# Output weights folded by 32-column products, epsilon as a 29th column, whole-bank gate steps: a linear-attention and GEGLU block

## The chip, the cores and the metric

One NeuronCore of a Trainium2 chip runs the whole program in one launch. The metric is the device time of one execution in microseconds (us); the kernel before took 190.51 us as a median of three runs (190.48 to 190.52). The profile is of one execution and counts from the first to the last instruction, its span.

## What is computed

A pre-norm attention block with linear attention and a gated feed-forward block, each with a residual, over 2048 tokens of 448 features. All inputs are bf16.

```python
def _A_ref(x, wqkv, wo):                     # B, S, D = 1, 2048, 448
    H = 16; Dh = D // H                      # 16 heads of 28
    q, k, v = split(x @ wqkv)
    phi = lambda t: jnp.where(t > 0, t + 1, jnp.exp(t)) + 1e-6
    pq, pk = phi(q), phi(k)
    kv = jnp.einsum("bhsd,bhse->bhde", pk, v)
    z = jnp.einsum("bhsd->bhd", pk)
    num = jnp.einsum("bhqd,bhde->bhqe", pq, kv)
    den = jnp.einsum("bhqd,bhd->bhq", pq, z)[..., None] + 1e-6
    return merge_heads(num / den) @ wo

def _B_ref(x, w_gate, w_up, w_down):         # Df = 1792
    h = _gelu(x @ w_gate) * (x @ w_up)
    return h @ w_down

h = x + _A_ref(_layernorm(x), A_wqkv, A_wo)
h2 = h + _B_ref(_layernorm(h), B_w_gate, B_w_up, B_w_down)
```

## The kernel before

The tokens are 16 tiles of 128. The program has three stages, all under one hand-made order.

**First stage, keys and queries.** Each tile is normalised, transposed (by PE for four tiles, by DMA for twelve) and multiplied by the key or the query weights (`k_t` and `q_t`, L469, four matmuls of 448 columns). Keys become `pk` on ACT and DVE (L480 to L482). The products `pt_t` (L488) accumulate the transposed normalised tile times `pk` over all tokens in four PSUM banks; a column of ones in the tile gives the sums `z`. The q groups are not all needed early: PE fills waits with them.

**Middle.** The sums leave PSUM: `z` to ACT (L514) and a copy to the other half of the partitions (L515, DVE), the four parts of `pt` by DVE (L516, L521) and ACT (L519). `kv` (L527) multiplies them by the value weights, 16 small matmuls. DVE masks the result head by head (`kvm`, L531) into a sheet of zeros and copies 64 columns of it once more (`kvd`, L536). Seven products (L547) of 128 columns of that sheet with the output weights give the folded weights `w2`: four groups of 128 rows, evicted by ACT (L551) and DVE (L553). Two DMAs also store them with the halves of the partitions exchanged. From then on the attention of a tile is one matrix product.

**The denominators.** DVE finishes the queries (L564 and L565 for a tile, L582 and L583 for a pair). The queries times `z` go to the tile `t1` (L569 or L585, mostly on POOL), DVE sums 28 columns per head (L572 or L586), ACT adds epsilon (L574 or L588), DVE inverts (L575 or L589) and scales the queries (L576 or L590). The first pair of tiles is transposed by PE and evicted by ACT (L599, L602), the others by DMA. `out1` (L617) multiplies the first pair by `w2`; `outA` and `outB` (L627, L628) do it for the other pairs on two halves of the array's rows.

**Feed-forward.** DVE adds the residual (L633), the second layer norm follows (L413, L414; L645 or L662), PE (L654) or DMA transposes. In `gu` steps, L731 (gate, lower 64 rows of the array) and L733 (up, upper 64 rows) run as pairs over seven pieces of the contraction. A step fills one PSUM bank of 512 columns for each: for the chunks of two tiles it has two 128-wide pieces of the hidden width and 256 tokens, for the chunks of four tiles one piece and 512 tokens. Two banks for each alternate. ACT takes the gelu of the bank in two halves (L751), DVE multiplies by the up product in two halves (L753). `down` steps (L697, L678) multiply by the down weights; DVE adds the residual (L707, L682) and SP stores (L708, L683). The last tile is done in two column halves, each with its own add and store.

**What sets the order.** Every operation is recorded as a task with the tasks that it waits for. `ORDERS` lists, for each engine, the task numbers in the order in which they are issued; an engine issues in that order, and a waiting instruction holds those behind it. `HOLD` names, for a task that waits for several others, which of the waits comes first. Both are tables of numbers, and both were written anew for the change because fewer tasks exist.

The lines on which the change bears:

```python
BK_KV, BK_W2 = 4, (5, 6, 7, 4)
gs = (c, c + 1) if c < 3 else (3,)          # w2: one or two products per group of 128 rows
for hh_ in range(2):                        # the gate and the product, a half bank each
```

Of the kernel before, what the change touches and what calls it, by code (L numbers as in the profile page):

```python
# [6 lines left out]
F32 = mybir.dt.float32  # L7
# [41 lines left out]
)  # L49
HOLD = {  # L50
    66: (36,), 141: (140,), 165: (164,), 214: (213,), 216: (215,), 323: (302,), 326: (324,), 431: (340,), 704:
    (564,), 735: (734,), 781: (672,), 839: (836,), 849: (846,), 854: (852,), 866: (865,),
# [176 lines left out]
def bass_sequential_preLN__linear_attn_block__glu_gated_geglu__prompt_kernel(  # L229
# [17 lines left out]
    G = _Graph()  # L247
    es = ExitStack()
    with es:
# [573 lines left out]
```

## Time and profile before

| what | value |
|---|---|
| median of three runs | 190.51 us (190.48 to 190.52) |
| span of the profiled execution | 188.3 us |
| granted clock of PE | 1.000 throughout |
| ACT gates (L751), 112 of 256 columns | 36.6 us, 383 ns each |
| DVE products (L753), 112 of 256 columns | 42.1 us, 416 ns each |
| PE gate and up matmuls (L731, L733), 490 each | 88.6 and 88.8 us, side by side |

The three runs carry no span of their own; the profiled execution's time is its span, and 2.2 us of the runs' median lie outside it. Busy time of PE counts overlapping tails of matmuls, so starts are read rather than lengths. Matmuls on 64 rows of the array appear as pairs at the same time. The rest of the profile is shown where the prediction reads it.

### The profile page before, as it was taken

The page shows a single profiled execution, that of the slowest core. Times are in us where ns is not written, and L with a number is a line of the kernel's source. Part 1 is how long each engine was busy: PE and PEld are TensorE (multiplying, and loading weights), DVE is VectorE, ACT ScalarE, POOL GpSimd, SP SyncE. Part 2 cuts the span into 40 slices and gives each one's busy share as a digit, 9 for nine tenths or more (in the row PEclk, how much of TensorE's full clock was granted, in tenths as well). Part 3 has the DMA queues.
Part 4 walks back from the last instruction along what each step waited for, and adds up shares of the span by engine and source line. Part 5 has one row for each costly group of instructions (what it writes and reads, how often), then busy time and mean ns, then how long its engine had stood idle before and what let it go on. Part 6 is the DMA issues. An engine that isn't in the chain of part 4 may idle for free.

```text
span 188.3 us, 4459 instructions
## 1 busy us (share of the span) xinstructions
PE 184.3 (98%) x1813; PEld 109.2 (58%) x1813; DVE 129.3 (69%) x330; ACT 76.5 (41%) x220; POOL 50.0 (27%) x91
## 2 busy tenths in 40 slices
PE   7999999999999999999999999999999999999994
PEld 7545555555688788965554555555545545454554
DVE  4999959999899998786796762562645244335432
ACT  3878752799963231432234222321242222224100
POOL 6067910704505686033614000206100000000000
PEclk9999999999999999999999999999999999999999
DMA  5996458999393526820005720000096000002024
GB/s 169 387 231 88 96 104 194 218 222 174 65 320 64 95 52 116 84 52 0 0 3 98 144 54 0 0 3 2 3 135 111 3 0 24 3 0 98 3 79 140
DMA packets 35076, 17.11 MB, mean 91 GB/s; under 512 B 26864, under 2 KB 33648, under 8 KB 35056
## 3 DMA queue, kind: packets, MB, share of 16 engines
q1 hardware_dynamic: 34432, 16.32, 41.1%
q10 hardware_dynamic: 624, 0.52, 0.8%
q8 instruction: 14, 0.23, 0.5%
q14 instruction: 6, 0.05, 0.1%
HBM read 8.26 MB, written 1.84 MB: 54 GB/s over the span
## 4 chain that ended last, share of the span: by engine, by line
PE 94%; DVE 3%; DMA 1%; issue 0%
PE ps L733 38%; PE ps L697 19%; PE ps L469 12%; PE ps L731 9%; PE ps L488 6%; PE ps L627 3%; PE ps L678 3%; PE ps L628 2%; DMA x_sb<-in_A_x_dram 1%; DVE st L413 1%; PE ps L617 1%; PE ps L547 1%; PE ps L527 1%; PE ps L443 0%; PE ps L654 0%; DVE den L572 0%
## 5 line engine op out<-in xcount | busy, mean ns | idle before, releaser
L733 PE MATMUL ps<-hnT,wgu_sb 64*128 64x512 bf16 (+1 forms) x490 | 88.8, 333 | 0.0
L731 PE MATMUL ps<-hnT,wgu_sb 64*128 64x512 bf16 (+1 forms) x490 | 88.6, 333 | 0.0
L751 ACT ACTIVATE gl<-ps 128x256 bf16<-128x256 f32 x112 | 36.6, 383 | 85.3 <-PE ps L731 84.4
L753 DVE TENSOR_TENSOR hh<-ps,gl 128x256 bf16<-128x256 f32 x112 | 42.1, 416 | 41.4 <-ACT gl L751 41.3
L733 PEld LDWEIGHTS ps<-hnT,wgu_sb 64*128 64x128 bf16 x490 | 45.2, 94 | 32.9 <-DVE hh L753 3.4
L731 PEld LDWEIGHTS ps<-hnT,wgu_sb 64*128 64x128 bf16 x490 | 45.4, 94 | 2.5
L697 PE MATMUL ps<-wd_sb,hh 64*128 64x448 bf16 x392 | 41.5, 349 | 0.0
L697 PEld LDWEIGHTS ps<-wd_sb,hh 64*128 64x128 bf16 x392 | 23.2, 94 | 14.5
L469 PE MATMUL ps<-wqk_sb,xnT 128*128 128x448 bf16 x128 | 27.4, 353 | 0.0
L413 DVE BATCH_NORM_STATS2 st<-x_sb 128x6 f32<-128x448 bf16 x32 | 19.2, 612 | 1.8 <-DMA x_sb<-in_A_x_dram 1.7
L585 POOL TENSOR_TENSOR t<-pq,zbc 128x448 f32<-128x448 bf16 x12 | 12.3, 1042 | 23.7 <-DVE pq L583 22.0
L469 PEld LDWEIGHTS ps<-wqk_sb,xnT 128*128 128x128 bf16 x128 | 11.9, 98 | 11.4 <-DVE pk L482 0.8
L488 PE MATMUL ps<-pk,xnn 128*128 128x448 bf16 x64 | 13.9, 352 | 0.0
L627 PE MATMUL ps<-w,pqnT 64*128 64x448 bf16 x49 | 11.5, 349 | 0.1
L425 POOL TENSOR_SCALAR ln<-mv 128x2 f32<-128x2 f32 x7 | 2.0, 291 | 35.2 <-DVE mv L414 35.0
L480 ACT ACTIVATE e<-ps 128x448 bf16<-128x448 f32 x16 | 8.5, 539 | 5.6 <-PE ps L469 5.5
L628 PE MATMUL ps<-pt_sb,pqnT 64*128 64x448 bf16 x42 | 10.2, 350 | 0.0
L633 DVE TENSOR_TENSOR x_sb<-ps,x_sb 128x448 bf16<-128x448 f32 x16 | 9.6, 616 | 0.7 <-PE ps L628 0.6
L662 POOL TENSOR_SCALAR hn<-x_sb,nm,rs 128x448 bf16<-128x448 bf16 x14 | 9.9, 719 | 0.4
L482 DVE SCALAR_TENSOR_TENSOR pk<-ps,e 128x448 bf16<-128x448 f32 x16 | 9.8, 617 | 0.1
L488 PEld LDWEIGHTS ps<-pk,xnn 128*128 128x128 bf16 x64 | 6.3, 98 | 5.9 <-DVE pk L482 0.3
L453 POOL TENSOR_SCALAR xnn<-x_sb,nm,rs 128x448 bf16<-128x448 bf16 x12 | 8.9, 744 | 2.2 <-ACT rs L422 1.9
(85 smaller groups left out, 160.5 us busy)
## 6 DMA issues: line engine op xcount, KB each, us to landing
out_dram<-x_sb SPq DMA_DIRECT2D x15, 112.0 KB, 1.8
wd_sb<-in_B_w_down_dram SPq DMA_DIRECT2D x1, 1568.0 KB, 8.4
x_sb<-in_A_x_dram SPq DMA_DIRECT2D x3, 448.0 KB, 5.9
wgu_sb<-in_B_w_gate_dram SPq DMA_DIRECT2D x1, 896.0 KB, 12.1
wgu_sb<-in_B_w_up_dram SPq DMA_DIRECT2D x1, 896.0 KB, 16.5
wgu_sb<-in_B_w_gate_dram SPq DMA_DIRECT2D x1, 672.0 KB, 6.1
wgu_sb<-in_B_w_up_dram SPq DMA_DIRECT2D x1, 672.0 KB, 8.5
wo_sb<-in_A_wo_dram SPq DMA_DIRECT2D x1, 392.0 KB, 7.5
```

The source lines that it names most:

```text
L413: op("dve", lambda e: e.bn_stats(st[:, t, :], src_ap), [b_src], [b_st[t]], "bnst%s_%d" % (tag, t))
L469: ins = e.matmul(ps[:, bk, 0:D], xnT[:, t, k, :], wqk_sb[:, k, c0:c0 + D], start=(k == 0), stop=(k == 3))
L488: ins = e.matmul(ps[:, BK_PT[c], 0:D], xnn[:, t % XN_R, c * 128:(c + 1) * 128], pk[:, ip, :], start=(t == 0), stop=(t == T - 1))
L585: op("pool", lambda e, n=n: e.tensor_tensor(t1[:, n, :], pq[:, a + n, :], zbc[:, :], ALU.mult), [b_pq[a + n]] + b_z, [b_t1[n]], "t1p_%d" % ...
L627: e.matmul(ps[:, BK_OUT[0], 0:D], pqnT[ra, i2, sg // 2, :], w2[ra, sg // 2, :], start=(sg == 0), stop=(sg == 5))
L628: ins = e.matmul(ps[:, BK_OUT[1], 0:D], pqnT[rb, i2, 3 + (sg + 1) // 2, :], (w2 if sg == 6 else w2s)[rb, sg // 2, :], start=(sg == 0), sto ...
L662: op("pool", lambda e, t=t, sh=sh: e.tensor_scalar(hn[:, sh, 0:D], x_sb[:, t, :], nm2[:, t:t + 1], rs2[:, t:t + 1], ALU.add, ALU.mult), [b ...
L697: ins = e.matmul(ps[:, bko[half][n], 0:D], hh[rows, j, sl[n]], wd_sb[rows, j, :], start=(j == 0 and (half == 0 or p == 6)), stop=(j == NJ ...
L731: first = e.matmul(psG[:, jj * N:(jj + 1) * N], wgu_sb[A_, k, j * 128:(j + 1) * 128], hnT[A_, ka_, c0:c0 + N], start=(k == 0), stop=(k == ...
L733: ins = e.matmul(psU[:, jj * N:(jj + 1) * N], wgu_sb[B_, k, j * 128:(j + 1) * 128], hnT[B_, kb_, c0:c0 + N], start=(k == 0), stop=(k == NK ...
L751: G.add("act", lambda e, gi=gi, cs_=cs_, psG=psG: e.activation(gl[:, gi, cs_], psG[:, cs_], AF.Gelu_apprx_tanh), r=[b_ps[BK_G[i]]], w=[b_g ...
L753: op("dve", lambda e, dst=dst, srcU=srcU, srcL=srcL: e.tensor_tensor(dst, srcU, srcL, ALU.mult), [b_ps[BK_U[i]], b_glh], [b_ar[j_][t % HR] ...
```

## The change

Five things change.

1. The output weights are folded by sixteen products of 32 columns of the masked sheet instead of seven of 128. Each writes 32 partitions of its bank, in one of four quarters q, and takes only the group g of heads that the quarter belongs to. The extra copy `kvd` falls away. The fourth group of rows is now computed for its lower half only, and POOL copies that half to the upper one (`w2dup`).
2. The tile `t1` has 29 columns per head. The 29th holds epsilon, written once at the start, so that the sum over 29 columns already has it. The ten ACT instructions that added epsilon are gone.
3. In the two-tile chunks the gate and the product take the whole bank of 512 columns at once (`geW`, `hmW`). The four-tile chunks keep their halves.
4. The last tile is cut at column 320 instead of 224.
5. The orders of all engines are written anew, with most differences between the keys' end and the four-tile chunks. The order of PE from there on is unchanged.

```diff
 ORDERS = (
-    " 615 657 620 625 630 635 682 704 683 699 714 709 636 719 724 641 734 729 642 739 744 749 754 759 764 769 781"
+    " 579 620 584 589 594 599 644 666 645 661 676 671 600 681 686 605 696 691 606 701 706 711 716 721 726 731 743"
...
 HOLD = {
-    66: (36,), 141: (140,), 165: (164,), 214: (213,), 216: (215,), 323: (302,), 326: (324,), 431: (340,), 704:
+    20: (19,), 32: (31,), 34: (33,), 35: (34,), 37: (34,), 41: (40,), 43: (42,), 44: (43,), 46: (43,),
...
-        t1 = sb("t1", [128, 2, D], F32)
+        t1 = sb("t1", [128, 2, H, DH + 1], F32)
...
-        op("pool", lambda e: e.memset(eps_d[:], EPS), [], [b_epsd], "epsd")
+        op("pool", lambda e: e.memset(t1[:, :, :, DH:DH + 1], EPS), [], [b_epsd], "epsd")
...
-        op("dve", lambda e: e.tensor_copy(kvz[:, 4 * D:4 * D + 64], kvz[:, 4 * D - 64:4 * D]), [b_kvm], [b_kvd], "kvd")
-
-        def kvc(g, c):
+
+        def kvc(g, c, q):
             o = g * D + c * 128 if c < 3 else 4 * D - 64
-            return kvz[:, o:o + 128]
-
-        for c in range(4):
-            def fw2(e, c=c):
-                gs = (c, c + 1) if c < 3 else (3,)
+            return kvz[:, o + 32 * q:o + 32 * q + 32]
+
+        for c, parts in enumerate((((0, 0), (1, 0), (2, 0), (3, 0), (3, 1)), ((0, 1), (1, 1), (2, 1), (3, 2)), ((0, 2), (1, 2), (2, 2), (3, 3), (2, 3)), ((0, 3), (1, 3)))):
+            def fw2(e, c=c, parts=parts):
                 ins = None
-                for g in gs:
-                    ins = e.matmul(ps[:, BK_W2[c], 0:D], kvc(g, c), wo_sb[:, g, :], start=(g == gs[0]), stop=(g == gs[-1]))
+                for i, (q, g) in enumerate(parts):
+                    ins = e.matmul(ps[32 * q:32 * q + 32, BK_W2[c], 0:D], kvc(g, c, q), wo_sb[:, g, :],
+                                   start=q not in [x[0] for x in parts[:i]], stop=q not in [x[0] for x in parts[i + 1:]])
                 return ins
...
+        G.add("pool", lambda e: e.tensor_copy(w2[B_, 3, :], w2[A_, 3, :]), r=[b_w2[3]], w=[b_w2t], name="w2dup")
...
-                    op("act", lambda e, i=i: e.activation(den[:, i, :], den[:, i, :], AF.Identity, bias=eps_d[:, 0:1]), [b_den[i], b_epsd], [b_den[i]], "deA_%d" % t)
...
-                op("act", lambda e: e.activation(den[:, i:i + 2, :], den[:, i:i + 2, :], AF.Identity, bias=eps_d[:, 0:1]), b_den[i:i + 2] + [b_epsd], b_den[i:i + 2], "deP_%d" % p)
...
-            parts = [(BK_L[t][0], 0, D)] if t < T - 1 else [(BK_L[t][0], 0, D // 2), (BK_L[t][1], D // 2, D)]
+            parts = [(BK_L[t][0], 0, D)] if t < T - 1 else [(BK_L[t][0], 0, 320), (BK_L[t][1], 320, D)]
...
-                for hh_ in range(2):
-                    cs_ = slice(hh_ * 256, (hh_ + 1) * 256)
+                for hh_ in range(2 if nj == 1 else 1):
+                    cs_ = slice(hh_ * 256, (hh_ + 1) * 256) if nj == 1 else slice(0, 512)
```

How the orders move, at the three places that the prediction speaks of. In the changed kernel the line numbers are higher (L564 became L636, L565 L637, L516 L588, L521 L593, L547 L616).

DVE, from the last key tile to the sums of the denominators; before:

```order
L482 SCALAR_TENSOR_TENSOR pk<-ps,e 128x448
L565 TENSOR_TENSOR pq<-pq,eq 128x448
L564 TENSOR_SCALAR eq<-eq 128x448
L516 CAST pt_sb<-ps 64x448
L515 COPY zbc<-zbc 64x448
L565 TENSOR_TENSOR pq<-pq,eq 128x448
L569 TENSOR_TENSOR t<-pq,zbc 128x448
L572 TENSOR_REDUCE den<-t 128x16
L521 CAST pt_sb<-ps 128x448
L575 RECIPROCAL rd<-den 128x16
```

and now:

```order
L554 SCALAR_TENSOR_TENSOR pk<-ps,e 128x448
L637 TENSOR_TENSOR pq<-pq,eq 128x448 x2
L588 CAST pt_sb<-ps 64x448
L587 COPY zbc<-zbc 64x448
L641 TENSOR_TENSOR t<-pq,zbc 128x16x28
L644 TENSOR_REDUCE den<-t 128x16
L593 CAST pt_sb<-ps 128x448
L646 RECIPROCAL rd<-den 128x16
```

The second addition of a query tile stood between the copy of `z` and the product with it; it now stands ahead of the first cast, and the first step of that query tile (L564) stands further ahead still, outside the piece.

PE, from the kv products to out1; before:

```order
L527 MATMUL ps<-pt_sb,wv_sb 112x112 x16
L469 MATMUL ps<-wqk_sb,xnT 128x448 x8
L547 MATMUL ps<-wo_sb,hh 128x448 x6
L469 MATMUL ps<-wqk_sb,xnT 128x448 x4
L547 MATMUL ps<-wo_sb,hh 128x448
L599 MATMUL ps<-ident,pqn 128x128 x8
L469 MATMUL ps<-wqk_sb,xnT 128x448 x4
L617 MATMUL ps<-w,pqnT 128x448 x8
```

and now:

```order
L599 MATMUL ps<-pt_sb,wv_sb 112x112 x16
L541 MATMUL ps<-wqk_sb,xnT 128x448 x8
L616 MATMUL ps<-wo_sb,hh 32x448 x16
L541 MATMUL ps<-wqk_sb,xnT 128x448 x4
L669 MATMUL ps<-ident,pqn 128x128 x8
L541 MATMUL ps<-wqk_sb,xnT 128x448 x4
L687 MATMUL ps<-w,pqnT 128x448 x8
```

The products of the output weights now stand in one piece; the q groups around them are partly of other tiles than before.

DVE, between the first pair's residual and the transposes of its layer norm; before:

```order
L633 TENSOR_TENSOR x_sb<-ps,x_sb 128x448 x2
L413 BN_STATS st<-x_sb 128x6 x2
L414 BN_AGGR mv<-st 128x2 x2
L586 TENSOR_REDUCE den<-t 128x32
L645 TENSOR_SCALAR hn<-x_sb,mv,rs 128x448 x2
L589 RECIPROCAL rd<-den 128x32
L647 COPY hn<-hn 128x64 x2
```

and now:

```order
L703 TENSOR_TENSOR x_sb<-ps,x_sb 128x448 x2
L485 BN_STATS st<-x_sb 128x6 x2
L486 BN_AGGR mv<-st 128x2
L653 TENSOR_SCALAR eq<-eq 128x896
L486 BN_AGGR mv<-st 128x2
L657 TENSOR_REDUCE den<-t 128x32
L715 TENSOR_SCALAR hn<-x_sb,mv,rs 128x448 x2
L659 RECIPROCAL rd<-den 128x32
L717 COPY hn<-hn 128x64 x2
```

A step on the queries of a later pair (L582 before, L653 now) has moved in between the two means.

More of the change, by code (lines that the diff above doesn't have):

```diff
@@ L618, in fout @@
                         return ins
-                    G.add("pe", fout, r=[(b_pqnT[i2][n], 0)] + [(b_w2[g], g) for g in range(NG)], w=[(b_ps[BK_OUT[n]], 0)], name="out1_%d" % (a + n), mw=True)
+                    G.add("pe", fout, r=[(b_pqnT[i2][n], 0)] + [(b_w2[g], g) for g in range(NG)] + [(b_w2t, 3)], w=[(b_ps[BK_OUT[n]], 0)], name="out1_%d" % (a + n), mw=True)
             else:
@@ L629, in foutp @@
                         return ins
-                    parts.append(G.add("pe", foutp, r=b_pqnT[i2] + b_w2 + b_w2s, w=[b_ps[b_] for b_ in BK_OUT], name="out%s_%d" % (part, p), sync=parts[-1:]))
+                    parts.append(G.add("pe", foutp, r=b_pqnT[i2] + b_w2 + b_w2s + [b_w2t], w=[b_ps[b_] for b_ in BK_OUT], name="out%s_%d" % (part, p), sync=parts[-1:]))
             for t in (a, a + 1):
@@ L679, in fnd @@
                     return ins
-                G.add("pe", fnd, r=[(b_ar[j][t % HR], j if j >= NJ - 2 else 0) for j in range(NJ)] + [b_wd], w=[b_ps[bk]], name="down%d_%d" % (c1 - c0, t), mw=True)
+                G.add("pe", fnd, r=[(b_ar[j][t % HR], j if j >= NJ - 2 else 0) for j in range(NJ)] + [b_wd], w=[b_ps[bk]], name="down%d_%d" % (D if t < T - 1 else D // 2, t), mw=True)
                 bo = b_x[t] if c0 == 0 else _Buf("xl")
-                op("dve", lambda e, t=t, psO=psO, c0=c0, c1=c1: e.tensor_tensor(x_sb[:, t, c0:c1], psO, x_sb[:, t, c0:c1], ALU.add), [b_ps[bk], b_x[t]], [bo], "fo%d_%d" % (c1 - c0, t))
+                op("dve", lambda e, t=t, psO=psO, c0=c0, c1=c1: e.tensor_tensor(x_sb[:, t, c0:c1], psO, x_sb[:, t, c0:c1], ALU.add), [b_ps[bk], b_x[t]], [bo], "fo%d_%d" % (D if t < T - 1 else D // 2, t))
                 G.add("sp", lambda e, t=t, c0=c0, c1=c1: e.dma_start(outv[:, t, c0:c1], x_sb[:, t, c0:c1]), r=[bo], name="do_%d" % t, kind="dma_out")
@@ L704, in b2_pair @@
                 if p == 6:
[L705 to L706 removed]
+                    xt, bx = t1f[:, n, :], b_t1[n]
+                    op("dve", lambda e, t=t, n=n: e.tensor_tensor(t1f[:, n, :], ps[:, bko[0][n], 0:D], x_sb[:, t, :], ALU.add), [b_ps[bko[0][n]], b_x[t]], [b_t1[n]], "fa448_%d" % t)
                 op("dve", lambda e, t=t, psO=psO, xt=xt: e.tensor_tensor(x_sb[:, t, :], psO, xt, ALU.add), [b_ps[bko[1][n]], b_x[t], bx], [b_x[t]], "fo448_%d" % t)
@@ L749, in gu_chunk @@
                         srcL = gl[:, gi, cs_].rearrange("p (a n) -> p a n", a=njh)
-                    b_glh = b_gl2[gi][hh_]
+                    b_glh = b_gl2[gi][hh_:] if nj > 1 else b_gl2[gi][hh_:hh_ + 1]
                     G.add("act", lambda e, gi=gi, cs_=cs_, psG=psG: e.activation(gl[:, gi, cs_], psG[:, cs_], AF.Gelu_apprx_tanh),
-                          r=[b_ps[BK_G[i]]], w=[b_glh], name="ge%d_%d" % (hh_, v), after=[tbl2])
+                          r=[b_ps[BK_G[i]]], w=b_glh, name="ge%s%d_%d" % ("W" if nj > 1 else "", hh_, v), after=[tbl2])
                     op("dve", lambda e, dst=dst, srcU=srcU, srcL=srcL: e.tensor_tensor(dst, srcU, srcL, ALU.mult),
-                       [b_ps[BK_U[i]], b_glh], [b_ar[j_][t % HR] for j_ in jr for t in th], "hm%d_%d" % (hh_, v))
+                       [b_ps[BK_U[i]]] + b_glh, [b_ar[j_][t % HR] for j_ in jr for t in th], "hm%s%d_%d" % ("W" if nj > 1 else "", hh_, v))
         done, t0, tbl2 = 0, 0, None
```

28 lines of the change are left out of this document (13 added, 15 removed), and 130 rows, old and new, of tables (HOLD, ORDERS).

## The prediction

> **What bounds the kernel now.** First the page: engine shares, and the chain of work that ended last.
>
> ```profile
> span 188.3 us, 4459 instructions
> ...
> PE 184.3 (98%) x1813; PEld 109.2 (58%) x1813; DVE 129.3 (69%) x330; ACT 76.5 (41%) x220; POOL 50.0 (27%) x91
> ...
> PE 94%; DVE 3%; DMA 1%; issue 0%
> ```
>
> PE is busy for 98% of the span, and 94% of the chain is PE. So only three things can move the time: a stretch in which PE stands, the number of matmul slots that PE has to run, and what lies behind the last matmul. All else matters only where it makes PE stand. Next the timeline of PE, and of its weight loads, around the folded output weights:
>
> ```profile
> 34.23 1.68 PE L469 MATMUL ps<-wqk_sb,xnT 128*128 128x448 bf16 x8
> 35.96 1.03 PE L527 MATMUL ps<-pt_sb,wv_sb 128*112 128x112 bf16 x16
> 36.83 1.68 PE L469 MATMUL ps<-wqk_sb,xnT 128*128 128x448 bf16 x8
> 38.34 1.30 PE L547 MATMUL ps<-wo_sb,hh 112*128 112x448 bf16 x6
> 40.24 0.35 PE L547 MATMUL ps<-wo_sb,hh 112*128 112x448 bf16 x1
> ```
>
> ```profile
> 35.96 0.33 PEld L527 LDWEIGHTS ps<-pt_sb,wv_sb 128*112 128x112 bf16 x5 [0.50 <-DVE pt_sb L521]
> ```
>
> A group's length includes the tail of its last matmul, so the pace is read from starts: eight of L469 from 36.83 to 38.34 are 0.189 us each, which I call a slot. The eight from 34.23 let go at 34.23 + 1.51 = 35.74, but the kv products (L527) start at 35.96. PE stands 0.22 us, and the last row names what it waited for, DVE's cast L521. The seven products of L547 are seven slots, 1.33 us.
>
> **The change part by part. (1) The wait of kv.** DVE's timeline ahead of it:
>
> ```profile
> 32.08 0.38 DVE L565 TENSOR_TENSOR pq<-pq,eq 128x448 bf16<-128x448 bf16 x1
> 32.38 0.27 DVE L564 TENSOR_SCALAR eq<-eq 128x448 bf16<-128x448 bf16 x1
> 32.73 0.62 DVE L516 CAST pt_sb<-ps 64x448 bf16<-64x448 f32 x1
> 33.37 0.39 DVE L515 COPY zbc<-zbc 64x448 f32<-64x448 f32 x1
> 33.79 0.39 DVE L565 TENSOR_TENSOR pq<-pq,eq 128x448 bf16<-128x448 bf16 x1
> 34.10 0.62 DVE L569 TENSOR_TENSOR t<-pq,zbc 128x448 f32<-128x448 bf16 x1
> 34.76 0.62 DVE L572 TENSOR_REDUCE den<-t 128x16 f32<-128x448 f32 x1
> 35.29 0.61 DVE L521 CAST pt_sb<-ps 128x448 bf16<-128x448 f32 x1
> ```
>
> The order now has two L565 ahead of L516, where L565 and L564 stood. Two at 0.30 (32.08 to 32.38) give DVE free at 32.68, still before L516's 32.73. Behind L515, L569 follows at once, 34.10 - 33.79 = 0.31 sooner; the reduce grows by 16 of 448 elements, 0.02. L521 then ends near 35.90 - 0.29 = 35.61, kv could start 0.06 later (35.96 - 35.90) at 35.67, and PE is free at 35.74. The 0.22 goes, with 0.07 of cover left. PE also takes a pt product of tile 14 earlier, but its input on DVE (L482) likewise moves ahead of two L565. Bounds: 0, since 0.3 of new lateness on DVE restores the wait, and 0.22. I take **-0.22**, because no instruction on this stretch of DVE is new.
>
> **(2) The output weights.** Seven products of 128 columns become sixteen of 32, four for each quarter of the columns, with the same 448 moving columns. If different quarters run side by side, one quarter's products run one after another, and starts keep the program's order (quarters 0123, 3012, 301, 0123, 2), they need five slots: 5 x 0.189 = 0.945. No row shows quarters. The nearest rows are the two halves of the rows, and what PE loses when the shape of its tiles changes:
>
> ```profile
> 48.13 0.50 PE L654 MATMUL ps<-ident,hn 128*128 128x128 bf16 x6
> 48.57 0.36 PE L627 MATMUL ps<-w,pqnT 64*128 64x448 bf16 x1
> 48.57 0.36 PE L628 MATMUL ps<-pt_sb,pqnT 64*128 64x448 bf16 x1
> ```
>
> ```profile
> 180.08 0.35 PE L697 MATMUL ps<-wd_sb,hh 64*128 64x448 bf16 x1
> 180.36 5.51 PE L678 MATMUL ps<-wd_sb,hh 128*128 128x448 bf16 x42
> ```
>
> L627 and L628 start together, so halves do run side by side. Six transposes with a tail of 0.22 take 0.50, 0.056 apart; the next start could be 48.47 and is 48.57: 0.10 lost. The last L697 starts at 180.08, its slot ends at 180.27, L678 starts at 180.36: 0.09. The new products stand together and cost two such changes, 0.19. The sum is 0.945 + 0.19 = 1.135 against 1.33: **-0.19**. Bounds: four slots and free changes, 0.76, a gain of 0.57; all sixteen in a row, 3.02 + 0.19 = 3.21, a loss of 1.88. The halves are the nearest rows, so I take side by side.
>
> The Trainium skill, "TensorE: Matmul & The Clock Gate", section "Measured speedup vs the span model", gives 2.38 times for three column tiles; an estimate from that page is 3.02 / 2.38 + 0.19 = 1.46, a term of +0.13, and 190.3 in all. The same page, section "The mechanism", lets a weight load overlap running matmuls only in another row group, which speaks against quarters that share all rows. This case's trace does not bear that out for the whole array, where L469 keeps its 0.189 although every matmul has a load of its own (1813 and 1813 on the page); for quarters no run shows it.
>
> The DVE copy L536 goes, and q groups that stood between the products move without new slots. The new 64x448 copy on POOL feeds the fourth matmul of out1 (L617); a 128x448 product there takes 1.04 (L585, below), and PE runs a q, the transposes and another q, 0.76 + 0.45 + 0.76, between the last product and out1. Nothing.
>
> **(3) Epsilon.** The view of groups, forms apart:
>
> ```profile
> L753 DVE TENSOR_TENSOR hh<-ps,gl 128x256 bf16<-128x256 f32 x112 | 42.1, 416 | 41.4 <-ACT gl L751 41.3
> L585 POOL TENSOR_TENSOR t<-pq,zbc 128x448 f32<-128x448 bf16 x12 | 12.3, 1042 | 23.7 <-DVE pq L583 22.0 <-DVE mv L414 1.7
> L588 ACT ACTIVATE den<-den,eps_d 128x32 f32<-128x32 f32 x6 | 1.9, 317 | 0.2 <-DVE den L586 0.2
> L551 ACT ACTIVATE w<-ps 128x448 bf16<-128x448 f32 x2 | 1.0, 541 | 0.0
> ```
>
> Ten instructions (L588 and L574) of at most 0.32 leave ACT, which is busy 41%; in the rows above PE waits for none of them: **0**. Should POOL be slower on 28 of 29 columns, L585 has 23.7 us of idle ahead of its twelve; one place is an exception, a rival below.
>
> **(4) Whole-bank gates.** One step in the two-tile part, and the same rows of PE later:
>
> ```profile
> 79.48 0.66 ACT L751 ACTIVATE gl<-ps 128x256 bf16<-128x256 f32 x2 [1.44 <-PE ps L731]
> 80.17 0.76 DVE L753 TENSOR_TENSOR hh<-ps,gl 128x256 bf16<-128x256 f32 x2 [0.23 <-ACT gl L751]
> 80.81 0.38 PE L731 MATMUL ps<-hnT,wgu_sb 64*128 64x512 bf16 x1
> 80.98 0.39 PE L733 MATMUL ps<-hnT,wgu_sb 64*128 64x512 bf16 x1
> ```
>
> ```profile
> 92.33 0.38 PE L731 MATMUL ps<-hnT,wgu_sb 64*128 64x512 bf16 x1
> 92.53 0.39 PE L733 MATMUL ps<-hnT,wgu_sb 64*128 64x512 bf16 x1
> ```
>
> A line through 256 columns (0.38, a pair's 0.66 less the 0.28 to its second start) and 448 (L551, 0.541) puts a gate of 512 at 0.59; one through L753's 0.416 and L521's 0.61 puts the product at 0.68. From 79.48 the new pair ends at 79.48 + 0.59 + 0.03 + 0.68 = 80.78, the old ended at 80.93. So the upper rows (L733), which start 0.17 behind the lower (L731) at 80.81, would lag 0.03. That looks like a gain. But the four-tile steps stay in halves and bring the lag back, 0.20 at 92.33; it is paid once, by the lone L697 at 180.08. So **0**; bounds a gain of 0.2 if the lag never returns, and a loss of 0.03 where three two-tile steps follow each other.
>
> **(5) What is late next** are the transposes L654:
>
> ```profile
> 47.06 0.20 DVE L647 COPY hn<-hn 128x64 bf16<-128x64 bf16 x2
> 47.69 0.28 PE L654 MATMUL ps<-ident,hn 128*128 128x128 bf16 x2
> ```
>
> They have 47.69 - 47.26 = 0.43 of cover, and PE now comes 0.41 sooner. Their chain starts at out1, also some 0.4 sooner, but the order puts a 128x896 instruction (L582; about 0.3) into it on DVE and one L497 on ACT. DVE alone would leave 0.1; ACT may use it up: **+0.03**, bounds 0 and 0.3.
>
> **(6) The tail.** The last tile's 224 + 224 columns become 320 + 128, the same for PE.
>
> ```profile
> 185.90 0.39 DVE L682 TENSOR_TENSOR x_sb<-ps,x_sb 128x224 bf16<-128x224 f32 x1 [0.95 <-PE ps L678]
> ```
>
> ```profile
> L682 DVE TENSOR_TENSOR x_sb<-ps,x_sb 128x448 bf16<-128x448 f32 x1 | 0.6, 625 | 1.6 <-PE ps L678 1.6
> ```
>
> ```profile
> out_dram<-x_sb SPq DMA_DIRECT2D x15, 112.0 KB, 1.8
> out_dram<-x_sb SPq DMA_DIRECT2D x2, 56.0 KB, 1.6
> ```
>
> 0.625 for 448 columns and 0.39 for 224 make 0.105 per 100, so the last add is 0.10 shorter. Its DMA falls from 56 to 32 KB; at 0.2 per 56 KB that is 0.09 at most, and I take half. The 320 piece is ready 14 x 0.056 = 0.78 before PE ends, and its add takes 0.49, so it is off DVE in time. **-0.15**, bounds 0 and -0.2.
>
> **Sum.** -0.22 - 0.19 + 0.03 - 0.15 = -0.53: the profiled span goes from 188.3 to 187.8. The median of the runs is 190.51, 2.2 above that span; with the same 2.2, **190.0 us**.
>
> **The rivals.** *The quarters run one behind another* (slower): halves of the rows are shown side by side, quarters of the columns, which all read the same 112 rows, never. It decides once the sixteen take 0.53 more than the forecast's 1.135; in full, 3.21 - 1.135 = 2.07 more, 192.1. Chance 0.13. *They overlap, but each slot shows its weight load*, as at a change of shape, 0.1: 5 x 0.1 = 0.5 more, 190.5. Chance 0.14; the page's rule on loads would do this. *DVE is late in the middle*: kv's 0.22 returns, or the transposes wait 0.3: 190.25. For it the covers of 0.07 and nearly none; against it that DVE gains no instruction there and loses L536. Chance 0.08. *POOL pays for the 28-of-29 stride* (slower): the first L585 pair feeds a reduce that stands, in DVE's order, ahead of what the transposes wait for; twice 1.04 more, less about 0.9 by which the pair now starts earlier (one L576 fewer ahead of it, and PE's 0.4), stops L654 for 1.1: 191.1. It decides from some 45% on each. Chance 0.08. *The upper rows' lag is cured*: 189.8, chance 0.07; the rows at 92.33 speak against it. The forecast has 0.50.
>
> **How the numbers follow.** A measurement of this kernel can tell about 0.2%, 0.38 us, from no change: under 190.13 is faster, over 190.89 slower. Faster: 0.45 of the forecast's 0.50, and the cured lag, 0.52. Within: the forecast's rest, the shown loads and the late DVE, 0.27. Slower: quarters in a row, and POOL, 0.21. The forecast's own range is 189.75 to 190.25; for 8 in 10 it reaches over the shown loads to POOL: 189.7 to 191.2.
>
> **What would show it.** Right: kv within 0.02 of the slot before it; sixteen products in about 0.95 with four starts together; no new gap of PE up to out1; a last add near 0.29. Wrong: products 0.189 apart throughout; weight loads of kv or of the transposes waiting for DVE; POOL's product well over 1.04; or no lone matmul ahead of L678.

## The result and the profile after

| kernel | median, lowest to highest (us) | ratio to before | span of the profiled run |
|---|---|---|---|
| before | 190.50 (190.38 to 191.01, 6 runs) | | 188.3 |
| changed | 191.97 (191.79 to 192.07, 6 runs) | 1.006, 95% interval 1.0041 to 1.0080 | 190.1 |
| forecast | 190.0 (range 189.7 to 191.2) | 0.997 | 187.8 |

The change makes the kernel slower by 1.47 us where 0.5 less was forecast; the time is 1.97 above the forecast and lies above its range. The page of the changed kernel, in the lines that were shown of before:

```profile
span 190.1 us, 4439 instructions
...
PE 184.8 (97%) x1822; PEld 114.1 (60%) x1822; DVE 129.9 (68%) x315; ACT 73.2 (39%) x196; POOL 53.8 (28%) x92
...
PE 87%; DVE 6%; DMA 3%; POOL 1%; SPq 1%; issue 0%; ACT 0%
```

PE's share of the chain that ended last fell from 94% to 87%; DVE's rose from 3% to 6%, and POOL is in it. PE's timeline of the changed kernel shows where it stands:

```profile
36.09 0.99 PE L599 MATMUL ps<-pt_sb,wv_sb 128*112 128x112 bf16 x16
36.91 1.68 PE L541 MATMUL ps<-wqk_sb,xnT 128*128 128x448 bf16 x8
38.81 0.94 PE L616 MATMUL ps<-wo_sb,hh 112*32 112x448 bf16 x16 [0.22 <-DVE hh L603]
39.68 0.93 PE L541 MATMUL ps<-wqk_sb,xnT 128*128 128x448 bf16 x4
40.97 0.62 PE L669 MATMUL ps<-ident,pqn 128*128 128x128 bf16 x8 [0.35 <-DVE w L624]
41.42 0.92 PE L541 MATMUL ps<-wqk_sb,xnT 128*128 128x448 bf16 x4
42.18 0.73 PE L687 MATMUL ps<-w,pqnT 128*128 128x448 bf16 x3
44.01 1.12 PE L687 MATMUL ps<-w,pqnT 128*128 128x448 bf16 x5 [1.10 <-POOL w L625]
```

The brackets count from the modelled tail of the matmul before; by starts the three pauses are longer. The eight query matmuls (L541) let go at 36.91 + 8 x 0.189 = 38.42, a change of shape takes 0.10, and the products (L616) could start at 38.52; they start at 38.81: **0.29** lost, to DVE's masking (L603). The four from 39.68 end at 40.44, the transposes (L669) start at 40.97: **0.53**, to DVE's eviction (L624). Three matmuls of out1 (L687) from 42.18 end at 42.75, the fourth starts at 44.01: **1.26**, to POOL's copy (L625). Together 2.08. The same stretch in the chain that ended last, in order of time (start, length, what):

```profile
36.91 1.31 DVE pqn L647
38.22 0.53 DVE hh L603
38.76 0.54 DVE den L644
39.30 0.53 DVE pqn L647
39.83 0.55 DVE den L644
40.38 1.07 DVE w L624 x2
...
41.50 2.47 POOL w L625
...
44.01 1.12 PE ps L687 x5
```

It is one chain with no more than 0.05 between two links: a scaling of the queries (L647), the masking, three more DVE steps, both evictions, the copy, out1. Its first and its last link before PE are far too long: another L647 in this list takes 0.53, and a POOL product of twice the partitions takes 1.04 (L585 before). The two engines' own timelines around the first one:

```profile
36.83 1.39 DVE L647 TENSOR_TENSOR pqn<-pq,rd 128x448 bf16<-128x448 bf16 x1
38.15 0.61 DVE L603 TENSOR_TENSOR hh<-ps,mask 112x448 bf16<-112x448 f32 x1
...
39.22 0.61 DVE L647 TENSOR_TENSOR pqn<-pq,rd 128x448 bf16<-128x448 bf16 x1
```

```profile
34.20 3.55 POOL L641 TENSOR_TENSOR t<-pq,zbc 128x448 f32<-128x448 bf16 x3 [8.56 <-DVE zbc L587]
41.50 2.46 POOL L625 COPY w<-w 64x448 bf16<-64x448 bf16 x1 [3.76 <-DVE w L624]
```

POOL's three products end at 34.20 + 3.55 = 37.75, and the long L647 ends 0.47 behind that, at 38.22. The copy ends at 43.96, 0.42 behind the last DVE step that ran beside it:

```profile
41.52 0.32 DVE L653 TENSOR_SCALAR eq<-eq 128x896 bf16<-128x896 bf16 x1
41.77 0.60 DVE L647 TENSOR_TENSOR pqn<-pq,rd 128x448 bf16<-128x448 bf16 x1
...
42.46 0.55 DVE L654 TENSOR_TENSOR pq<-pq,eq 128x896 bf16<-128x896 bf16 x1
42.94 0.60 DVE L647 TENSOR_TENSOR pqn<-pq,rd 128x448 bf16<-128x448 bf16 x1
```

So theory A: a DVE instruction that reads two operands from SBUF and a POOL instruction that reads SBUF keep each other out; in the first case POOL had the place and DVE stood, in the second the other way round. The rivals: each is slow for a reason of its own (B for L647; for the copy, that it goes across halves of the partitions).

### The profile page after: what moved, and what is told of

Its sections match the earlier page's. It is cut to its first block, busy times and chain, and to the rows that moved or that the text cites. A ratio compares the mean times of both kernels' runs of the same rounds, so it can differ in the third digit from the quotient of the medians.

```text
span 190.1 us, 4439 instructions
## 1 busy us (share of the span) xinstructions
PE 184.8 (97%) x1822; PEld 114.1 (60%) x1822; DVE 129.9 (68%) x315; ACT 73.2 (39%) x196; POOL 53.8 (28%) x92
## 4 chain that ended last, share of the span: by engine, by line
PE 87%; DVE 6%; DMA 3%; POOL 1%; SPq 1%; issue 0%; ACT 0%
PE ps L803 38%; PE ps L767 19%; PE ps L541 9%; PE ps L801 8%; PE ps L560 4%; DMA x_sb<-in_A_x_dram 3%; PE ps L748 3%; PE ps L697 3%; PE ps L698 2%; POOL w L625 1%; DVE den L644 1%; DVE pqn L647 1%; SPq L418 1%; DVE pk L554 1%; DVE st L485 1%; PE ps L687 1%
## 5 line engine op out<-in xcount | busy, mean ns | idle before, releaser
L823 DVE TENSOR_TENSOR hh<-ps,gl 128x256 bf16<-128x256 f32 (+1 forms) x98 | 41.1, 455 | 41.7 <-ACT gl L821 41.3
L821 ACT ACTIVATE gl<-ps 128x256 bf16<-128x256 f32 (+1 forms) x98 | 35.5, 414 | 88.0 <-PE ps L801 87.1
L767 PEld LDWEIGHTS ps<-wd_sb,hh 64*128 64x128 bf16 x392 | 25.3, 94 | 12.4
L541 PE MATMUL ps<-wqk_sb,xnT 128*128 128x448 bf16 x128 | 27.7, 353 | 0.1
L541 PEld LDWEIGHTS ps<-wqk_sb,xnT 128*128 128x128 bf16 x128 | 12.0, 98 | 12.0 <-DVE pk L554 1.1
L656 POOL TENSOR_TENSOR t<-pq,zbc 128x448 f32<-128x448 bf16 x12 | 12.8, 1079 | 20.2 <-DVE den L657 12.4
```

The costliest lines, as they stand in the source:

```text
L541: ins = e.matmul(ps[:, bk, 0:D], xnT[:, t, k, :], wqk_sb[:, k, c0:c0 + D], start=(k == 0), stop=(k == 3))
L656: op("pool", lambda e, n=n: e.tensor_tensor(t1[:, n, :, 0:DH], pq[:, a + n, :].rearrange("p (h d) -> p h d", h=H), zbc[:, :].rearrange("p ...
L767: ins = e.matmul(ps[:, bko[half][n], 0:D], hh[rows, j, sl[n]], wd_sb[rows, j, :], start=(j == 0 and (half == 0 or p == 6)), stop=(j == NJ ...
L821: G.add("act", lambda e, gi=gi, cs_=cs_, psG=psG: e.activation(gl[:, gi, cs_], psG[:, cs_], AF.Gelu_apprx_tanh), r=[b_ps[BK_G[i]]], w=b_gl ...
L823: op("dve", lambda e, dst=dst, srcU=srcU, srcL=srcL: e.tensor_tensor(dst, srcU, srcL, ALU.mult), [b_ps[BK_U[i]]] + b_glh, [b_ar[j_][t % HR ...
```

## The experiments

Runs 1 to 5 are the changed kernel with the edit shown; runs 6 to 9 and 12 go on from run 5, run 10 from run 3. Orders are told by instructions, as they follow each other on the engine. Without the copy (runs 2, 3 and 10) most line numbers are one lower.

### 1. The masking first

```diff
 L646 RECIPROCAL rd<-den 128x16
-L647 TENSOR_TENSOR pqn<-pq,rd 128x448
 L603 TENSOR_TENSOR hh<-ps,mask 112x4x112
+L647 TENSOR_TENSOR pqn<-pq,rd 128x448
```

> The changed kernel with one step moved on DVE: the masking of kv (L603) stands ahead of the first scaling of the queries (L647) instead of behind it. Theory A (two engines block each other): in the changed kernel that L647 ran from 36.83 to 38.22, 1.39 us where its like take 0.56 to 0.61, because a POOL product (L641, to 37.74) was running, and 37.74 + 0.48 is its end. Both read two operands from SBUF. Then with the masking first, at 37.14 to 37.76, the POOL product is over when L647 starts; L647 takes 0.6, the output weights start 0.28 sooner, the transposes L669 no longer wait 0.53 for DVE, and the POOL copy (L625) still makes out1 wait about 1.3, since both sides of that wait move by about 0.8. Time about 191.97 - 0.8 = 191.2. Rival B (L647 is slow there for a reason of its own): it still takes 1.4, only the 0.28 is won, 191.7. Rival C (the start of the run, not the middle, is what is late): no change, 192.0.

Measured 191.41 us (191.19 to 191.48), ratio 1.0040 (1.0026 to 1.0055). DVE, then PE of this kernel:

```profile
36.99 0.62 DVE L603 TENSOR_TENSOR hh<-ps,mask 112x448 bf16<-112x448 f32 x1 [0.20 <-PE ps L599]
37.53 0.61 DVE L647 TENSOR_TENSOR pqn<-pq,rd 128x448 bf16<-128x448 bf16 x1
```

```profile
39.27 0.93 PE L541 MATMUL ps<-wqk_sb,xnT 128*128 128x448 bf16 x4
40.35 0.62 PE L669 MATMUL ps<-ident,pqn 128*128 128x128 bf16 x8 [0.16 <-DVE w L624]
```

POOL's three products end at 34.07 + 3.56 = 37.63 here, 0.02 behind the masking, and the same scaling, which follows the masking, takes 0.61: rival B falls. The wait of the products is gone; the transposes still wait 40.35 - 39.27 - 0.76 = 0.32, so of the 0.8 expected 0.56 came. The wait ahead of out1 stays at 1.26 (42.14 to 43.40). A start of the run that is late (rival C) is ruled out as the cause of this part.

### 2. No copy

```diff
-... ((0, 3), (1, 3)))):
+... ((0, 3), (1, 3), (2, 3), (3, 3)))):
...
-            rows = slice(0, 128) if c < 3 else A_
+            rows = slice(0, 128)
...
-        G.add("pool", lambda e: e.tensor_copy(w2[B_, 3, :], w2[A_, 3, :]), r=[b_w2[3]], w=[b_w2t], name="w2dup")
```

> The changed kernel without the POOL copy (L625): two more products of 32 columns write the upper half of the fourth group of output weights, eighteen in all, and its eviction takes all 128 rows. Theory (the copy is what out1 waits for): the wait of 1.28 us ahead of out1's fourth matmul goes, the two products add one slot of 0.19 (the third and fourth quarter then have five), 191.97 - 1.28 + 0.19 = 190.9. Rival (out1 would wait anyway, for the transposed queries, whose second eviction ends at 42.49, or the late eviction at 41.43): out1 starts no sooner than 0.8 after that, the gain is 0.5 or less, 191.5 to 192.0.

Measured 190.66 us (190.37 to 191.41), ratio 1.0010 (0.9996 to 1.0024): 1.31 less than the changed kernel, expected 1.1. Eight matmuls of out1 now stand in one row without a pause. The rival, that out1 would wait anyway, falls.

### 3. Both

> Both edits: the masking of kv ahead of the first scaling, and no POOL copy. If theory A and the theory of the copy both hold, the gains add: 191.97 - 0.8 - 1.28 + 0.19 = 190.1, below the kernel before by 0.2%, and the rest to my forecast of 190.0 is the start of the run. If PE, now some 1.9 us sooner at out1 and at the transposes of the second norm, meets new waits there, 190.4 to 190.8.

Measured 190.31 us (189.98 to 190.81), ratio 0.9987 (0.9974 to 1.0000). The gains add: 0.56 + 1.31 = 1.87 expected from the two results, 1.66 found. What is left of the waits is 0.14 ahead of the transposes (40.30 after four matmuls from 39.40):

```profile
39.40 0.93 PE L540 MATMUL ps<-wqk_sb,xnT 128*128 128x448 bf16 x4
40.30 0.62 PE L668 MATMUL ps<-ident,pqn 128*128 128x128 bf16 x8
```

### 4. The copy by itself

```diff
 L646 RECIPROCAL rd<-den 128x16
-L653 TENSOR_SCALAR eq<-eq 128x896
-L647 TENSOR_TENSOR pqn<-pq,rd 128x448
 L646 RECIPROCAL rd<-den 128x16
-L654 TENSOR_TENSOR pq<-pq,eq 128x896
-L647 TENSOR_TENSOR pqn<-pq,rd 128x448
 L703 TENSOR_TENSOR x_sb<-ps,x_sb 128x448
+L653 TENSOR_SCALAR eq<-eq 128x896
+L647 TENSOR_TENSOR pqn<-pq,rd 128x448
+L654 TENSOR_TENSOR pq<-pq,eq 128x896
+L647 TENSOR_TENSOR pqn<-pq,rd 128x448
```

> The changed kernel with four DVE steps (L653, two L647, L654), which ran on DVE while the POOL copy (L625) was under way, moved behind the first residual (L703); DVE then has only short instructions of one operand until out1. The copy took 2.46 us and ended 0.42 after the last of those DVE steps. Theory A (DVE instructions with two operands in SBUF keep POOL out): the copy takes 0.4 to 0.6 us and out1's wait of 1.28 goes; what is late afterwards (the four steps) may cost as much again, so the time itself says little. Rival (the copy across halves of the partitions costs 2.46 in itself): it still takes 2.3 to 2.5 and out1 still waits 1.2.

POOL of this kernel:

```profile
41.85 0.55 POOL L625 COPY w<-w 64x448 bf16<-64x448 bf16 x1 [3.76 <-DVE w L624]
```

0.55 against 2.46, with nothing changed but the place of four DVE steps: the copy across halves is cheap, and what made it long was DVE. Out1 waited for nothing. The time, 192.77 in one run, is higher, since the four steps came late for what follows (0.9 of waiting at the transposes of the second norm, 0.5 for ACT).

### 5. Two moves on DVE, the copy kept

If only two operands from SBUF keep POOL out, it is enough to give DVE another step while the copy runs. (The copy here also names, as one of its waits, a POOL product that stands ahead of it; POOL had been idle for 2.77 us when the copy began.)

```diff
-L647 TENSOR_TENSOR pqn<-pq,rd 128x448
 L603 TENSOR_TENSOR hh<-ps,mask 112x4x112
+L647 TENSOR_TENSOR pqn<-pq,rd 128x448
 L644 TENSOR_REDUCE den<-t 128x16
 L647 TENSOR_TENSOR pqn<-pq,rd 128x448
-L644 TENSOR_REDUCE den<-t 128x16
 L624 CAST w<-ps 128x448
 L624 CAST w<-ps 64x448
+L644 TENSOR_REDUCE den<-t 128x16
```

> The changed kernel, its POOL copy (L625) kept, with two moves on DVE: the masking of kv (L603) ahead of the first scaling (L647), and the fourth sum of the denominators (L644, one operand, 0.63) from ahead of the two evictions L624 to behind them, so that it is what DVE does while the copy runs; the copy now waits for the POOL product before it by name. Theory A (only DVE instructions with two operands in SBUF keep POOL out): the evictions run at about 39.1 to 40.3, the copy beside L644 in about 0.55, done by 40.9, out1 waits for nothing, and the transposes L669 wait less than the 0.33 of the kernel with the masking alone. 191.41 (that kernel) - 1.27 - 0.3 = 189.8, under the forecast of 190.0 and under the kernel before by 0.3%. Rival (any work of DVE slows the copy): it takes over 1.2 beside L644 and is still held by L647 behind it, out1 waits again, 190.4 to 191.2.

Measured 190.47 us (190.37 to 190.99), ratio 0.9995 (0.9984 to 1.0007): as fast as the kernel before, 0.7 slower than expected. DVE, POOL and PE:

```profile
40.29 0.62 DVE L644 TENSOR_REDUCE den<-t 128x16 f32<-128x464 f32 x1
...
40.99 0.47 DVE L653 TENSOR_SCALAR eq<-eq 128x896 bf16<-128x896 bf16 x1
```

```profile
40.43 0.78 POOL L625 COPY w<-w 64x448 bf16<-64x448 bf16 x1 [2.77 <-DVE w L624]
```

```profile
41.27 1.68 PE L687 MATMUL ps<-w,pqnT 128*128 128x448 bf16 x8
42.78 4.70 PE L541 MATMUL ps<-wqk_sb,xnT 128*128 128x448 bf16 x24
47.77 0.95 PE L724 MATMUL ps<-ident,hn 128*128 128x128 bf16 x14 [0.29 <-DVE hn L717]
```

The copy is done at 41.21 and out1 waits for nothing, so a sum beside it does not keep it out. But "only two operands" is too narrow: L653 reads one, met the copy at 40.99, and both ran longer, 0.47 and 0.78, where they take 0.33 and 0.55 apart (run 12). All three pauses are gone, and yet the time is not 189.8, because a new one stands later: the 24 query matmuls from 42.78 are done at 47.32, and the transposes of the second norm (L724) wait 0.45 for DVE's wraps (L717). The windows view (length, then busy time of PE, its loads, DVE, ACT, POOL); first this kernel, then before:

```profile
37.00:50.00 13.00, 12.65 (x98) 6.50 (x98) 12.98 (x30) 12.07 (x29) 4.44 (x5) 1.00 0.86 163
```

```profile
37.00:50.00 13.00, 12.94 (x91) 7.06 (x91) 12.73 (x31) 12.58 (x33) 3.39 (x4) 1.00 0.87 162
```

DVE is busy for 12.98 of these 13 us. Theory D: with the waits gone, DVE's work from the masking to the second norm sets the middle, and what PE saves there is only waited away. ACT is nearly as full (12.07, and 12.58 before), so these shares alone do not show which of the two it is; runs 9 and 12 bear on that.

### 6 to 8. Single parts undone in the kernel with the two moves

Half-bank gates again (`for hh_ in range(2)`, as before):

> The kernel with the two moves, with the gates and products of the two-tile chunks in halves again, as before the change. Term (4) of the prediction: no difference, within 0.2 of the kernel with the two moves. Rivals: whole banks gain (this one slower by 0.2 or more, with a lone down matmul or a gap in PE that the other does not have), or they lose (this one faster by as much).

Products of 128 columns again:

```diff
-            return kvz[:, o + 32 * q:o + 32 * q + 32]
+            return kvz[:, o:o + (128 if c < 3 else 64)]
...
-                    ins = e.matmul(ps[32 * q:32 * q + 32, BK_W2[c], 0:D], kvc(g, c, q), wo_sb[:, g, :],
...
+                    ins = e.matmul(ps[0:128 if c < 3 else 64, BK_W2[c], 0:D], kvc(g, c, 0), wo_sb[:, g, :], start=(g == gs[0]), stop=(g == gs[-1]))
```

> The kernel with the two moves, with the output weights again by seven products of 128 columns (64 for the last) instead of sixteen of 32; the copy stays. By the trace of the changed kernel, sixteen products run in four slots and cost 0.87 with the change of shape behind them and 0.1 ahead, against 1.33: this one should be 0.36 slower than the kernel with the two moves. By the prediction's five slots, 0.19 slower. Rival (the wait of the transposes for DVE behind them takes it up): no difference.

The last tile cut at 224 again:

```diff
-            parts = [(BK_L[t][0], 0, D)] if t < T - 1 else [(BK_L[t][0], 0, 320), (BK_L[t][1], 320, D)]
+            parts = [(BK_L[t][0], 0, D)] if t < T - 1 else [(BK_L[t][0], 0, D // 2), (BK_L[t][1], D // 2, D)]
```

> The kernel with the two moves, with the last tile cut at 224 again instead of 320. Term (6): 0.15 slower, 0.10 of it a longer last add (0.39 against 0.29) and 0.05 the transfer behind it. Rivals: 0.10 (only the add), or nothing (the end is set by something that both share). Too small for the medians; read from the end of the last add to the end of the span, and from the start of the last tile's matmuls to that end.

| kernel | median | ratio to before |
|---|---|---|
| two moves (5) | 190.47 | 0.9995 (0.9984 to 1.0007) |
| and half-bank gates (6) | 190.47 | 0.9995 (0.9981 to 1.0010) |
| and wide products (7) | 190.56 | 1.0003 (0.9989 to 1.0018) |
| and even tail (8) | 190.85 | 1.0006 (0.9991 to 1.0022) |

The gates make no difference that these medians can tell, as term (4) had it. PE with the wide products:

```profile
38.39 1.71 PE L617 MATMUL ps<-wo_sb,hh 112*128 112x448 bf16 x7
39.94 0.92 PE L541 MATMUL ps<-wqk_sb,xnT 128*128 128x448 bf16 x4
```

They take 39.94 - 38.39 = 1.55: seven slots, 1.33, and 0.22 for two changes of shape, as one of the seven is 64 columns wide here. The sixteen take 0.97 (rows in run 12). The time is the same within what can be told: L724 starts without a wait, at 47.95, 11.90 behind kv, where run 5 has 11.78 with the wait. That is the rival of this run, and what theory D says. The even tail: the last add takes 0.39 against 0.29, and 1.99 against 1.89 pass from its end to the end of the span, 0.20 in all. Spans are given to 0.1, so this second part is known to some 0.05.

### 9 and 10. The second norm ahead of the next pair

```diff
-L486 BN_AGGR mv<-st 128x2
-L653 TENSOR_SCALAR eq<-eq 128x896
-L486 BN_AGGR mv<-st 128x2
-L657 TENSOR_REDUCE den<-t 128x32
+L486 BN_AGGR mv<-st 128x2 x2
+L653 TENSOR_SCALAR eq<-eq 128x896
 L715 TENSOR_SCALAR hn<-x_sb,mv,rs 128x448 x2
-L659 RECIPROCAL rd<-den 128x32
 L717 COPY hn<-hn 128x64 x2
+L657 TENSOR_REDUCE den<-t 128x32
+L659 RECIPROCAL rd<-den 128x32
```

> The kernel with the two moves, with DVE and ACT steps moved at the second norm: the scalings and wraps of the first pair (L715, L717) ahead of the sum (L657, 1.08) that stood before them, the two means (L486) next to each other, the logarithms (L492) next to each other on ACT ahead of a query step (L569), and a short reciprocal (L646) ahead of L653. Theory D (once out1 no longer waits, DVE's chain to the transposes L724 sets the middle): in the kernel with the two moves PE stood about 0.45 there (a q group that paces 1.21 against 0.757); the wraps then end about 0.8 sooner and the wait goes: 0.45 less, 190.0. Rival E (what is pushed back is late next): the sum and the scaling behind it (L657, L660) end 0.8 later, their transposes by DMA reach outA of the second pair late, and PE stands there instead, 190.3 to 191.0.

> The kernel with eighteen products and no POOL copy, with the same moves: the masking first, the fourth sum behind the evictions, and the steps of the second norm. It has one slot of 0.19 more than the kernel before in this list, and DVE's L653 is not held by the copy (0.33 against 0.47). Theory D: 0.05 to 0.2 slower than that kernel, 190.1 to 190.2. If the DVE chain is still the limit, they are equal.

The diff is that of run 9 on DVE; run 9 also moves L646 and, on ACT, L492, as its expectation says. Measured 191.70 (ratio 1.0056, 1.0039 to 1.0073) and 191.55 (1.0054, 1.0039 to 1.0069), against 190.0 and 190.1 to 190.2 expected. The wait at L724 shrank to 0.04 and to nothing, but what stands behind it on DVE came late, and not where rival E had put it: the eviction L730 of the transposed norm, for which the first gate step waits. The rows are of run 9.

```profile
46.67 0.70 DVE L715 TENSOR_SCALAR hn<-x_sb,mv,rs 128x448 bf16<-128x448 bf16 x2 [0.66 <-ACT rs L494]
...
50.97 0.62 DVE L730 COPY hnT<-ps 128x896 bf16<-128x896 bf16 x1
```

```profile
51.64 0.28 PE L801 MATMUL ps<-hnT,wgu_sb 64*128 64x256 bf16 x1 [1.28 <-DVE hnT L730]
```

The first row says why the move gained so little: the scalings (L715), now ahead of the sum (L657), wait 0.66 for ACT's step L494, and DVE stands. Counted from kv, they begin 0.36 sooner than in run 5 (46.67 - 36.36 against 46.66 - 35.99), and the sum and all behind it, L730 among them, come later: L730 by 1.12 (50.97 - 36.36 against 49.48 - 35.99). So DVE was not full here, and these two runs show the chain to L724 through DVE and ACT together rather than DVE alone. That the two kernels, 0.19 of PE's work apart, agree within 0.15 fits a limit outside PE.

### 11. The kernel before once more

> The kernel before, profiled once more, for the start of the run: its kv products began at 35.96, 0.22 of it a wait, and in the nine profiles of the changed kernel and its variants they begin between 35.91 and 36.97 without one. If the start varies from one execution to the next in every kernel, this profile gives 36.0 to 37.0; if the kernel before starts sooner by some 0.3 always, 35.9 to 36.0 again.

```profile
36.19 1.03 PE L527 MATMUL ps<-pt_sb,wv_sb 128*112 128x112 bf16 x16
```

36.19, where the first profile had 35.96: the start varies by more than 0.2 in the kernel before too, so a late start is not something that the change is shown to bring, and two profiles of before do not rule it out either. Here too PE is free 0.22 sooner (its eight query matmuls start at 34.46 and let go at 35.97). Spans of single profiles carry that variation; the medians decide.

### 12. Less work for DVE

```diff
-            if c % 2 == 0:
+            if c != 3:
                 op("act", lambda e, c=c, rows=rows: e.activation(w2[rows, c, :], ps[rows, BK_W2[c], 0:D], AF.Identity), [b_ps[BK_W2[c]]], [b_w2[c]], "evwA_%d" % c)
```

One of the two evictions goes from DVE to ACT: the one that frees the bank that the transposes write. Two more steps change places, L568 on ACT and L646 on DVE, as the expectation says, so it is not one step alone that is tested.

> The kernel with the two moves, with one of DVE's two evictions of the output weights (L624, 0.61) on ACT instead (L622, behind its first one), a query step of ACT (L568) moved behind the evictions of the transposes (L672), and a short reciprocal (L646) ahead of L653. Nothing else is moved. Theory D (with out1's wait gone, the sum of DVE's work from the masking to the second norm sets the middle): DVE loses 0.53 ahead of the transposes L724, where PE stood 0.45; the q group ahead of them paces 0.76 instead of 1.21 and the evictions behind them are sooner too: 190.47 - 0.45 = 190.0. Rival F (the wait goes over to ACT, which gains 0.54 there): the query products L541 or out1 wait for ACT's steps on the queries or L672, 0.2 to 0.6, and the time stays at 190.4 to 190.6.

Measured **190.10 us** (189.66 to 190.37, 9 runs) against 190.61 for the kernel before beside it, ratio 0.9966 (0.9951 to 0.9981): faster than before and than run 5. PE and POOL:

```profile
34.50 1.68 PE L541 MATMUL ps<-wqk_sb,xnT 128*128 128x448 bf16 x8
36.02 0.99 PE L599 MATMUL ps<-pt_sb,wv_sb 128*112 128x112 bf16 x16
36.84 1.68 PE L541 MATMUL ps<-wqk_sb,xnT 128*128 128x448 bf16 x8
...
39.32 0.93 PE L541 MATMUL ps<-wqk_sb,xnT 128*128 128x448 bf16 x4
40.17 0.74 PE L669 MATMUL ps<-ident,pqn 128*128 128x128 bf16 x8
40.75 0.92 PE L541 MATMUL ps<-wqk_sb,xnT 128*128 128x448 bf16 x4
...
43.02 4.70 PE L541 MATMUL ps<-wqk_sb,xnT 128*128 128x448 bf16 x24
47.63 0.95 PE L724 MATMUL ps<-ident,hn 128*128 128x128 bf16 x14
```

```profile
39.96 0.55 POOL L625 COPY w<-w 64x448 bf16<-64x448 bf16 x1 [2.29 <-DVE w L624]
```

The 24 query matmuls from 43.02 are done at 47.56, and L724 starts at 47.63: 0.07 instead of 0.45. Rival F took a little: L669 runs over 0.58 instead of 0.44 and starts 0.09 late, some 0.2 in all. What is left, 0.17, is what theory D is shown to be worth here: L724 stands 11.61 behind kv, against 11.78 in run 5, and that although ACT has one eviction more. Another 0.15 between the two profiles lies in the feed-forward, where run 5 has a pause of 0.14 that run 12 does not have (below).

## Why the prediction was wrong

**The step that failed** stands in term (2): "a 128x448 product there takes 1.04 (L585, below), and PE runs a q, the transposes and another q, 0.76 + 0.45 + 0.76, between the last product and out1. Nothing." Both halves of it fail. The price of the copy was taken from POOL as if POOL were alone; beside DVE's two-operand steps it is 2.46 (alone 0.55, run 4). And its start was counted from the last product, as if the eviction it copies came at once; that eviction stands behind five other steps on DVE, the masking first among them, and ends at 41.43, just ahead of the copy's start at 41.50, 1.75 behind the end of the products (38.81 + 0.94). Of the two the price decided: at 1.04 the copy would have ended at 42.54, before PE was ready for the fourth matmul at 42.75, since PE was late as well. The two together cost 1.26 of the 1.97 us by which the time is above the forecast; without the copy, run 2 is 1.31 faster.

The trace of before had the sign of it, in a row that the prediction left unread:

```profile
34.27 3.39 POOL L569 TENSOR_TENSOR t<-pq,zbc 128x448 f32<-128x448 bf16 x3 [8.83 <-DVE pq L565]
```

Three products in 3.39 are 0.27 more than three at 1.04, and DVE's own L569, from 34.10 to 34.72, covers the first one's start.

The Trainium skill, "SBUF — State Buffer", section "Who interferes with whom", states the mechanism: a VectorE instruction with both inputs in SBUF and a GpSimd instruction that reads SBUF contend for one shared pair of ports, which is an exclusive lock. Runs 1 and 4 agree (0.61 against 1.39, 0.55 against 2.46). It adds that the order of issue decides who is blocked; here the copy began at 41.50 by the profile, ahead of L653 (41.52) and L647, and was held through both and beyond, so the recorded starts do not show who had the place. They are 0.02 apart, and starts on POOL are rough.

The other steps:

- **The rival "DVE late in the middle"** happened, but at another place and dearer: 0.29 + 0.53 = 0.82, not 0.25. The words "against it that DVE gains no instruction there" looked at the number of instructions; one scaling (L647) had moved ahead of the masking, and POOL's product stood in its way. The order of DVE that the prediction went by ends just short of it. Run 1 takes 0.50 of the 0.82 off; the other 0.32 is the sum (L644) ahead of the evictions, and goes in run 5.
- **(1) The wait of kv**: right. In run 12 the eight query matmuls from 34.50 end at 36.01 and kv starts at 36.02; in none of the twelve profiles of the changed kernel and its variants does kv wait, in both of before it waits 0.22. But kv starts no earlier for it: at 35.91 to 36.98, against 35.96 and 36.19, since PE comes to it later. How much of the 0.22 is time gained is not shown.
- **(2) The products**: right in kind, too small. The quarters run side by side, in four slots rather than five: in run 12 from 36.84 + 1.51 = 38.35 to 39.32, 0.97 with both changes of shape, against 1.33, so -0.36 for -0.19. The sixteen start in four groups of four, at 38.45, 38.65, 38.84 and 39.02; by the program's order, which the prediction's five slots kept, the third four would hold quarter 0 twice. They do not keep it: the fifth product, the first that reports its end, is the eighth to start. Neither quarters in a row nor shown loads occurred.
- **(3) Epsilon**: right, 0. The POOL product of 28 of 29 columns takes 1.079 for 1.042.
- **(4) Gates**: right, 0 (run 6). A gate of 512 columns takes 0.598 and its product 0.684 in the changed kernel, for 0.59 and 0.68.
- **(5) The transposes of the second norm**: +0.03 with 0.3 as the upper bound. In the changed kernel it is 0, because PE comes too late to wait there: luck. Once the three pauses are gone it is 0.45 (run 5), above the bound, and run 12 takes it off.
- **(6) The tail**: right, -0.20 for -0.15 by runs 5 and 8, -0.16 in the changed kernel's profile (table below).

The POOL product of the changed kernel, in the view of groups:

```profile
L656 POOL TENSOR_TENSOR t<-pq,zbc 128x448 f32<-128x448 bf16 x12 | 12.8, 1079 | 20.2 <-DVE den L657 12.4 <-DVE pq L654 7.6
```

The sum with the measured sizes is -0.22 - 0.36 - 0.20 + 2.08 = +1.30, and +1.47 was measured. The profiles say where the time went, each part from the start of one group on PE to the start of the next:

| profile | to kv | kv to L724 (before: L654) | to L748 (before: L678) | to the end |
|---|---|---|---|---|
| before | 35.96 | 11.73 | 132.67 | 7.94 |
| changed | 36.09 | 13.42 | 132.81 | 7.78 |
| two moves (run 5) | 35.99 | 11.78 | 132.91 | 7.72 |
| eviction on ACT (run 12) | 36.02 | 11.61 | 132.76 | 7.71 |

The middle of the changed kernel is longer by 1.69, which is 2.08 of pauses less 0.36 for the products, within 0.03. The runs that list both have 1.8 to 2.1 between span and time, not the 2.2 that the forecast added, so the profile of before is of an execution some 0.2 faster than its median. In run 5 the 0.36 that PE saves there is gone again in the wait of 0.45 at L724, and the tail's gain in a feed-forward that takes 0.24 more. So even with the pauses gone the forecast would have been missed by about 0.5 (190.47 for 190.0), though inside its range: DVE and ACT have little slack in the middle (12.73 and 12.58 of 13.00 us busy in before), and term (5) had +0.03 for that. Still open is the feed-forward: its 0.14 in the changed kernel is a pause in one gate step (158.03, where the pace gives 157.90). The same pause is in runs 1 to 3, 5 and 7 to 10, but not in before or in runs 4, 6 and 12; no row names what it waits for.

## What to carry to other kernels

Price a new instruction on POOL by what DVE does beside it, not by POOL's time alone, and count when its input is ready by the queue of the engine that makes it. Before counting a saving of the busiest engine, look at the busy time of its partners in that stage: where the window is nearly full, as with DVE's 12.73 of 13.00 here, the saving can become a wait (run 5), and it may take a step off the partner to keep it (run 12). A full window does not say which partner it is: run 9, which put DVE's scalings ahead of its sum, ran into ACT.

## What the runs showed of the hardware

- A POOL copy of 64x448 bf16 from the lower to the upper half of the partitions takes 0.55 alone and beside a DVE sum (L644); beside four DVE steps, three of them with two operands in SBUF, it took 2.46. In the other direction a DVE step of 0.61 took 1.39 beside a POOL product.
- A DVE step of one operand (L653, 128x896 bf16) that met the copy took 0.47 instead of 0.33, and the copy 0.78 instead of 0.55 (run 5 against run 12); a sum (L644) beside a copy kept its 0.62.
- Matmuls of 32 output columns in four quarters of the columns, with the same 448 moving columns, run four at a time: sixteen in 0.97 us with two changes of shape, where seven of 128 columns take 1.33. Their starts do not keep the program's order (run 12).
